# A fused sparse-attention and squared-ReLU kernel: first loads on two queues, wider mask matmuls, a re-weighted instruction planner and a last output cut by columns

## The chip, the cores and the metric

The kernel runs on one core of a Trainium2 chip. A core has a matmul engine (TensorE, "PE" in the profile, with its weight loads listed apart as "PEld"), three engines for elementwise work (VectorE "DVE", ScalarE "ACT", GpSimd "POOL") and SyncE ("SP"), which here only issues transfers. [...] semaphores order the engines against one another. The metric is device time in microseconds (us), the median of repeated executions.

## The reference

Eight batches of eight heads, 576 positions, head width 64. Half of the heads see only the last 32 positions, the other half every position with the same remainder modulo 32. The result, one row per position, goes through two matrices with s·relu(h)²+b between them.

```python
scores = scale * np.matmul(q, k.transpose(0, 1, 3, 2))
mask_local = (rel >= 0) & (rel < stride)
mask_strided = (rel >= 0) & (pos[None, :] % stride == pos[:, None] % stride)
attn = softmax(np.where(mask, scores, -1e9))     # local for heads 0-3, strided for 4-7
x = np.matmul(attn, v).transpose(0, 2, 1, 3).reshape(4608, 512)
r = np.maximum(x @ w_in, 0.0)                    # w_in 512 x 2048
out = (s * (r * r) + b) @ w_out                  # w_out 2048 x 512
```

## The kernel before

**Tiling.** Attention is done for pairs of heads: `pair_steps(b, m)`, batch `b`, pair `m` of four; pairs 0 and 1 are local, 2 and 3 strided. A pair is a list of small PE steps: transposes of q and k (L494, L502), scores (L623) with six or eight tiles, the product with v (L684), and in the early batches a transpose back (L731). Between them stand copies out of the accumulators, the exponential on ACT (L641), reciprocals and scaling (L701, L711). The first matrix product (`ff1`, L983) takes tiles of 512 tokens, nine in all, and so does the second (`ff2`, L1238, for tiles 0 and 1; `ff2_seven`, L951, for the others, which needs seven products of half matrices where eight would be usual). The last two tiles use a seven-product scheme for the first matrix as well (`ff1_seven`, L1208).

**Order of the work.** The order of instructions is made by a planner that runs when the program is built. `Plan` holds a clock and, for every piece of data, the time at which it expects it. PE steps are taken one after the other: attention steps when attention is behind its schedule (`due`, with the offset `ahead`), else `ff1` or `ff2`. Work for ACT, DVE, POOL and the transfer queues is posted and released in `flush`, in the order of the time when its data are expected plus a weight by kind (the dictionary `ORDER`; its entry `SLACK` says how far an engine's list may run ahead). What the planner expects of a transfer is an estimate: `AT` gives the landing times of the first batch, `landing` those of later ones. A wrong estimate does not make the result wrong; it puts an instruction too early into an engine's list, where it waits for its data and everything behind it waits too.

**Head of the program.** Until the first q has landed, PE runs filler matmuls (`keep_running`, L1502). SP issues the identity, two heads of the v of batch 0 in fp32 (`stage_v`, L311, into the memory that later holds `w_out_sb`) and the mask table `negs` (L315). POOL issues q, k, the other v and the weights (L345, L372, L1365, L394), converts the staged v (L404) and then goes on issuing. In batch 0 (`PE_MASK = 1`) the mask is added to the scores by PE: before each score tile, a matmul of the identity with the table writes -30000 where nothing may be seen (L620), and the score matmul accumulates on it.

**v of later batches.** `fetch_v` issues the transfers (L382, L387) and enters when the planner expects them. `rows_before` posts a copy of 32 rows within `v_loc` (L404), on ACT or DVE, whichever the planner thinks free.

**End of the program.** The last product of the last tile is P3 in `ff2_seven`. Its two token halves (t = 0 and 1) have an accumulator bank each (`Ws`); `store` scales a half into an output tile `o` on DVE (L882) and SP issues its transfer (L886).

Of the kernel before, what the change touches and what calls it, by code (L numbers as in the profile page):

```python
# [18 lines left out]
class Plan:  # L19
# [22 lines left out]
    def post(self, needs, cost, fn, keys, lat=None):  # L42
        self.pend.append((needs, cost, fn, keys, lat))

    def flush(self):
        while True:
            best = None
            for p in self.pend:
                r = self.ready_at(p[0])
                if r is None or r > self.t:  # L50
                    continue
                if p[1].keys() <= {"A", "V"} and min(
                        self.free[e] for e in p[1]) > self.t + self.SLACK:
                    continue
                k = p[3][0]
                w = r + self.LATER.get(k[0] if isinstance(k, tuple) and k[2:3] != (0,) else None, 0.0)
                if best is None or w < best[0]:
                    best = (w, r, p)
            if best is None:
                return  # L60
            _, r, p = best
            self.pend.remove(p)
            eng = min(p[1], key=lambda e: max(self.free[e], r) + p[1][e])
            end = max(self.free[eng], r, self.t - self.SLACK) + p[1][eng]
            self.free[eng] = end
            p[2](eng)
            for k in p[3]:
                if isinstance(k, Group):
                    self.banks[k.name] = end + self.LAT[eng]
                    k = ("rel", k)  # L70
                soon = isinstance(k, tuple) and k[0] == "soon"
                self.done[k] = end + (6000.0 if soon else p[4] or self.LAT[eng])
# [45 lines left out]
class Step:  # L118
    def __init__(self, fn, ns, needs=(), group=None, keys=(), posts=(), after=None):
# [3 lines left out]

ORDER = {"g": 1500.0, "S": 2500.0, "in": 2500.0, "w_mix": 0.0, "wc": 1000.0, "ev": 1000.0,
         "c21": 1500.0, "c11": 500.0, "c12": 500.0, "C22": -1500.0, "fv": 0.0, "Vb": -400.0,
         "x": -1500.0, "Ub": 1000.0, "xc": -1500.0, "fe": -400.0, "k": 1500.0, "fu": -1500.0,
         "Va": 500.0, "p": 0.0, "c22": 500.0, "Ua": 2500.0, "e": -1500.0, "q": 0.0, "r": 0.0,
         "u": 0.0, "SLACK": 600.0, "ahead": 0.05}
KINDS = ("g", "S", "in", "w_mix", "wc", "Va", "Ua", "Ub", "Vb", "C22", "xc", "q", "k", "r", "x", "e",
         "p", "u", "ev", "fv", "fu", "fe", "c11", "c22", "c21", "c12")  # L130


def varied(order, rnd):

    order = dict(order)
    for kind in rnd.sample(KINDS, rnd.choice((1, 2, 4))):
        order[kind] = rnd.choice((-1500.0, -800.0, -400.0, 0.0, 500.0, 1000.0, 1500.0, 2500.0))
    if rnd.random() < 0.2:
        order["SLACK"] = rnd.choice((400.0, 600.0, 800.0, 1000.0))
    if rnd.random() < 0.2:  # L140
        order["ahead"] = rnd.choice((0.0, 0.05, 0.1, 0.2))
    return order

# [45 lines left out]
def lay_out(ctx, tc, nc, q, k, v, moe_w_in, moe_w_out, moe_s, moe_b, out, order, q_shape, out_shape,  # L189
# [112 lines left out]
    def v_band(b, h):  # L302

        return v[b, h].rearrange("(t p) d -> p t d", p=LQ)
# [4 lines left out]
    def stage_v(heads):  # L309
        for h in heads:  # L310
            nc.sync.dma_start(out=vl_stage[LPAD:128, h], in_=v_band(0, h))  # L311

# [135 lines left out]
    PE_MASK = 1  # L448
# [25 lines left out]
    def pair_steps(b, m):  # L474
# [135 lines left out]
        def score(i, group):  # L610
# [3 lines left out]
            def f():  # L614
                if i % per_s == 0:
                    st["s", g] = bank(group)
                c = i % per_s * 2 * nq
                if b < PE_MASK:

                    nc.tensor.matmul(  # L620
                        out=st["s", g][0:nk, c:c + 2 * nq], lhsT=ident[0:nk, 0:nk],
                        rhs=neg_loc if loc else neg_str, start=True, stop=False)
                nc.tensor.matmul(  # L623
                    out=st["s", g][0:nk, c:c + 2 * nq], lhsT=(st["k"][:, i * nq:i * nq + nk] if loc else st["k"][:, i, 0:SQ]),
                    rhs=st["q"][:, i].rearrange("d e c -> d (e c)"), start=b >= PE_MASK, stop=True)

            s = Step(f, (2 if b < PE_MASK else 1) * (2 * nq / 2.4 + 8), needs=[("q", id_), ("k", id_)],
                     group=group if i % per_s == 0 else None)
            if i % per_s == n - 1:
# [28 lines left out]
            return s  # L658

        gr = None  # L660
        for i in range(nt):
            if i % per_s == 0:
                gr = group_of("s", b, m)
            steps.append(score(i, gr))

# [187 lines left out]
    def ff2_seven(T):  # L853
# [23 lines left out]

        def store(i, k, of, plus, ts=slice(0, 2)):
            def g(eng):
                o = op.tile([128, 2, 256], FP32, tag="o", name="o")  # L880
                src = gts[of, T][:, ts] if (of, T) in gts else gts[of, T, ts.start]
                nc.vector.scalar_tensor_tensor(  # L882
                    out=o[:, ts], in0=src, scalar=s_sb[:, 0:1],
                    in1=plus()[:, ts], op0=ALU.mult, op1=ALU.add)
                r0 = T * PS + 256 * i
                nc.sync.dma_start(  # L886
                    out=out[r0:r0 + 256, 256 * k:256 * k + 256].rearrange(
                        "(t p) m -> p t m", p=128)[:, ts], in_=o[:, ts])
            return g
# [50 lines left out]
        for key, group, name, fresh, lhs, rhs, needs, more, posts in seq:  # L940
            for t in range(2):
                for k in range(H):
                    halves = last and name == "W"

                    def f(k=k, t=t, group=group, name=name, fresh=fresh, lhs=lhs, rhs=rhs, key=key,
                          halves=halves):
                        if halves and fresh and k == 0:
                            gts[name, T, t] = bank(Ws[t])[:, None, 0:256]
                        elif fresh and t == k == 0:
                            gts[name, T] = bank(group).rearrange("p (t m) -> p t m", t=2)  # L950
                        nc.tensor.matmul(out=gts[name, T, t][:, 0] if halves else gts[name, T][:, t],  # L951
                                         lhsT=lhs(k, t), rhs=rhs(k),
                                         start=fresh and k == 0 and (halves or t == 0),
                                         stop=t == 1 and k == H - 1, skip_group_check=True)
                    s = Step(f, 110, needs=needs(k) + ([(x[0], T, t) if halves and x == d("C22")
                                                        else x for x in more]),
                             group=(Ws[t] if halves else group) if fresh and k == 0 and
                             (halves or t == 0) else None)
                    if k == H - 1 and key == "P3" and last:
                        s.keys = [("P3", T, t)]  # L960
                        s.posts = [([("P3", T, t)], {"V": 420.0},
                                    store(0, 1, "W", val("Ub"), slice(t, t + 1)),
                                    [Ws[t]])]
                    elif t == 1 and k == H - 1:
                        s.keys = [d(key)]
                        s.posts = posts
                    if t == 1 and k == H - 1 and key == "P3":
                        s.keys = s.keys + [("F2", T)]
# [370 lines left out]
    def fetch_v(b):  # L1339
        load_vl(b)  # L1340
        plan.done["raw", "vl", b] = landing(4600)
        for mm in range(2):
            rows_before(b, mm, ("raw", "vl", b))
        if b < LONG_V:
            early_v(b)
        else:
            load_vs(b)
            arrive(both("vs", b), landing(5000))

# [10 lines left out]
    def after_landing(i, src):  # L1360
# [9 lines left out]
    plan.free["V"] = 6500.0  # L1370
    AT = {"ql0": 5200.0, "kl0": 6900.0, "ql1": 7850.0, "kl1": 8700.0, "qs": 10200.0,
          "ks": 12100.0, "vl0": 7100.0, "vl1": 13450.0, "vs": 15000.0}
    for key, at in AT.items():
# [7 lines left out]
    nc.sync.dma_start(out=sb_row[0:1, 1:2], in_=moe_b[None, :])  # L1381
    plan.done["sb_row",] = 16000.0
    def weights_in(eng):

        nonlocal ring
        nc.gpsimd.tensor_copy(out=gate[0:8, 2:3], in_=loaded[0, "qs"][64:SQ, 0:1])
        load_w_in()
        ring = 13200.0
        for keys, cost in ([0], 2700), ([1], 2500), ([2], 2500), ([3], 2500):
# [125 lines left out]
    def due():  # L1515

        pos = f1_pos[i1] + (f2[i2 - 1].pos if i2 else 0.0) + plan.ahead
        return (pos if pos <= 1 else 1 + (pos - 1) / 2) * batch_ns

    while i2 < len(f2) or any(at_i[p] < len(att[p]) for p in range(len(att))):  # L1520
        plan.flush()
# [14 lines left out]
        if i2 < len(f2):  # L1536
            order.append(2)
        if len(order) == 2 and i1 % 4 == 0 and f1_pos[i1] > (f2[i2 - 1].pos if i2 else 0.0) + 1:
            order.reverse()
# [56 lines left out]
```

## Time and profile before

| | |
|---|---|
| median of 3 runs | 298.67 us (298.17 to 298.99) |
| the profiled execution: its own time, its span | 298.86 us, 297.1 us |
| PE busy, matmuls | 290.5 us (98%), 2802 |
| DVE, ACT, POOL busy | 235.3, 194.3, 93.7 us |
| PE clock granted | 0.999 of full |
| transferred | 38.19 MB, mean 129 GB/s |

The span goes from the first to the last instruction; 1.8 us of the execution's time lie outside it. PE is shown as busy nearly always, but its busy time is modelled and overlapping, so idle PE time is better read from the starts of consecutive matmuls: a 128x256 matmul in a dense stretch starts 109 ns after the one before, a 128x512 one 216 ns. "issue" in the chain of waits is time in which the engine waits for nothing that the profile shows.

### The profile page before, as it was taken

To read this page: it belongs to the slowest core of one execution; us is meant where nothing else is said; L and a number is where in the kernel's file an instruction comes from. 1 tells how busy PE (TensorE), PEld (TensorE's weight loads), DVE (VectorE), ACT (ScalarE), POOL (GpSimd) and SP (SyncE) were. 2 spreads that over 40 slices of the span, in tenths; PEclk is the share of its full clock that TensorE was granted. 3 is DMA by queue.
4 is the path that set the end of the run, shared out by engine and by line. 5 is a ranking of instruction groups with operands and counts; after the bars stand their busy time and mean duration, and the time that the engine had idled before them with its cause. 6 is when DMAs were issued, how large, how long until landed. Compare 5 with 4: busy or idle time off the path is not lost.

```text
span 297.1 us, 7092 instructions
## 1 busy us (share of the span) xinstructions
PE 290.5 (98%) x2802; PEld 220.0 (74%) x2802; DVE 235.3 (79%) x501; ACT 194.3 (65%) x336; POOL 93.7 (32%) x140
## 2 busy tenths in 40 slices
PE   8999999999999999999999999999999999999995
PEld 3775656666556568889767776768888989999984
DVE  5857888798966988787877896759898588888963
ACT  3577957898838798647774878469877545675400
POOL 8873624601980296009710394100000000000000
PEclk9999999999999999999999999999999999999999
DMA  8999999997999499989999999999230300110214
GB/s 136 189 206 203 218 180 184 223 171 119 109 195 149 67 132 138 170 173 122 148 136 144 182 170 105 143 140 207 44 97 0 108 29 9 71 38 3 95 48 142
DMA packets 106152, 38.19 MB, mean 129 GB/s; under 512 B 85414, under 2 KB 103974, under 8 KB 106118
## 3 DMA queue, kind: packets, MB, share of 16 engines
q0 software_dynamic: 60848, 18.23, 62.7%
q1 hardware_dynamic: 45270, 19.51, 36.0%
q8 instruction: 22, 0.36, 0.5%
q14 instruction: 12, 0.10, 0.1%
HBM read 36.99 MB, written 10.62 MB: 160 GB/s over the span
## 4 chain that ended last, share of the span: by engine, by line
PE 88%; DMA 6%; ACT 2%; DVE 2%; POOL 1%; issue 1%; ACTq 0%
PE ps_f L983 28%; PE ps_f L951 22%; PE ps_f L1238 8%; DMA v_loc<-in_v_dram 6%; PE ps_s L623 5%; PE ps_f L1208 3%; PE ps_a L684 3%; PE ps_s L1502 2%; PE ps_a L1208 2%; PE ps_s L951 2%; PE ps_t L1208 2%; PE ps_s L1208 2%; PE ps_t L951 1%; PE ps_s L1238 1%; PE ps_t L684 1%; PE ps_t L502 1%
## 5 line engine op out<-in xcount | busy, mean ns | idle before, releaser
L983 PE MATMUL ps_f<-xT,w_in_sb 128*128 128x512 f16 (+4 forms) x568 | 115.5, 331 | 0.3 <-ACT u L1009 0.3
L1009 ACT ACTIVATE u<-ps_f 128x512 f16<-128x512 f32 x104 | 61.0, 594 | 32.5 <-PE ps_f L983 31.8
L983 PEld LDWEIGHTS <-w_in_sb 128*128 128x128 f16 x576 | 57.4, 114 | 23.2 <-issue 0.5
L951 PEld LDWEIGHTS <-gT 128*128 128x128 f16 x608 | 58.4, 98 | 9.2
L951 PE MATMUL ps_f<-w_out_sb,gT 128*128 128x256 f16 x376 | 55.6, 273 | 0.0
L1017 ACT ACTIVATE gT<-u 128x1024 f16<-128x1024 f16 x29 | 30.7, 1057 | 0.8
L1238 PE MATMUL ps_f<-w_out_sb,gT 128*128 128x512 f16 x112 | 30.4, 379 | 0.0
L951 PE MATMUL ps_f<-w_mix,gT 128*128 128x256 f16 x176 | 25.1, 273 | 0.0
L641 ACT ACTIVATE p_str<-ps_s 72x432 f16<-72x432 f32 (+1 forms) x46 | 20.7, 482 | 6.4 <-PE ps_s L623 5.8
L711 DVE TENSOR_TENSOR x_nat<-ps_a,rec 96x384 f16<-96x384 f32 (+2 forms) x46 | 24.1, 523 | 0.6
L641 ACT ACTIVATE p_loc<-ps_s 128x384 f16<-128x384 f32 x46 | 21.4, 494 | 4.8 <-PE ps_s L623 4.3
L1019 DVE TENSOR_TENSOR gT<-u 128x1024 f16<-128x1024 f16 x27 | 18.5, 686 | 5.9 <-ACT u L1009 5.4
L819 DVE TENSOR_TENSOR gT<-gT 128x1024 f16<-128x1024 f16 x34 | 22.4, 678 | 0.6 <-ACT gT L1017 0.4
L382 POOL DMA_DIRECT2D v_loc<-in_v_dram x24 | 17.7, 757 | 8.6 <-DMA w_out_sb<-in_moe_w_out_dram 5.7
L951 PEld LDWEIGHTS <-S 128*128 128x128 f16 x176 | 17.1, 98 | 2.9
L1238 PEld LDWEIGHTS <-gT 128*128 128x128 f16 x128 | 11.4, 98 | 7.8
L387 POOL DMA_DIRECT2D v_str<-in_v_dram x16 | 13.0, 816 | 12.3 <-PE ps_f L983 3.6
L684 PEld LDWEIGHTS <-p_str 72*128 72x128 f16 x256 | 12.8, 98 | 5.1 <-ACT p_str L641 0.4
L1323 POOL COPY gate<-kT 1x1 f16<-1x1 f16 x6 | 1.5, 256 | 45.0 <-DMA kT<-ks 45.0
L951 PE MATMUL ps_f<-w_mix,S 128*128 128x256 f16 x112 | 15.5, 273 | 0.0
L701 DVE RECIPROCAL rec<-ps_a 96x6 f32<-96x6 f32 (+2 forms) x47 | 8.6, 182 | 8.6 <-PE ps_a L684 8.4
L1149 ACT ACTIVATE gT<-u 128x1024 f16<-128x1024 f16 x12 | 12.7, 1058 | 1.7 <-DVE u L1128 1.4
(237 smaller groups left out, 529.7 us busy)
## 6 DMA issues: line engine op xcount, KB each, us to landing
out_dram<-o SPq DMA_DIRECT2D x34, 256.0 KB, 2.9
w_in_sb<-in_moe_w_in_dram POOLq DMA_DIRECT2D x4, 512.0 KB, 9.7
w_out_sb<-in_moe_w_out_dram POOLq DMA_DIRECT2D x4, 512.0 KB, 9.9
qs<-in_q_dram POOLq DMA_DIRECT2D x6, 288.0 KB, 8.4
ks<-in_k_dram POOLq DMA_DIRECT2D x6, 288.0 KB, 9.7
v_loc<-in_v_dram POOLq DMA_DIRECT2D x24, 72.0 KB, 9.6
ql<-in_q_dram POOLq DMA_DIRECT2D x4, 288.0 KB, 9.0
kl<-in_k_dram POOLq DMA_DIRECT2D x16, 72.0 KB, 3.6
```

What stands on the lines that cost most here:

```text
L382: nc.gpsimd.dma_start(out=vl[LPAD:128, h, :, 0:D], in_=v_band(b, h))
L641: nc.scalar.activation(out=st["pw", g][0:nk, 0:2 * n * nq], in_=st["s", g][0:nk, 0:2 * n * nq], func=AF.Exp, scale=scale)
L684: nc.tensor.matmul(out=st["pa", g][:, n % 6, :], lhsT=st["pw", gp_][0:nk, i * nq:i * nq + WIDE], rhs=vt[0:nk, 2 * mm + e, j, :])
L711: nc.vector.tensor_tensor(out=x_at(0, cnt), in0=st["pa", g][0:nq, 0:cnt, 0:D], in1=st["rec", g][0:nq, 0:cnt].to_broadcast([nq, cnt, D]), o ...
L819: {"V": nc.vector, "P": nc.gpsimd}[eng].tensor_tensor(out=at(out), in0=at(x), in1=at(y), op=op)
L951: nc.tensor.matmul(out=gts[name, T, t][:, 0] if halves else gts[name, T][:, t], lhsT=lhs(k, t), rhs=rhs(k), start=fresh and k == 0 and (ha ...
L983: nc.tensor.matmul(out=gts["h", T, ft][:, lo:hi], lhsT=w_in_sb[ft // 4][:, ct].rearrange("p (x l) -> p l x", l=4)[:, ft % 4], rhs=xT[ct][: ...
L1009: nc.scalar.activation(out=u, in_=gts["h", T, ft], func=AF.Relu)
L1017: nc.scalar.activation(out=g, in_=u, func=AF.Square)
L1019: nc.vector.tensor_tensor(out=g, in0=u, in1=u, op=ALU.mult)
L1208: nc.tensor.matmul(out=st[bk][:, 256 * t:256 * t + 256], lhsT=lhs(t, c), rhs=rhs(c), start=fresh and t == c == 0, stop=t == c == 1, skip_g ...
L1238: nc.tensor.matmul(out=gts[id_], lhsT=gts[T][:, ft, ts * 128:(ts + 1) * 128], rhs=w_out_sb[:, ft, cols], start=(ft == 0), stop=(ft == NFT ...
```

## The change

1. `stage_v`: head 0 of the staged v is issued from ACT's queue, head 1 stays on SP and so follows the identity directly; the mask table follows it.
2. Mask matmuls of batch 0: a new step `forbid` writes the mask of a whole accumulator bank at once (two local tiles, three strided ones), and stands ahead of the first score of that bank. It needs the table, neither q nor k. There are 12 of them where there were 28.
3. `fetch_v`: for the last batch alone the planner expects v 5 us later than before.
4. The last P3: the second token half is computed and stored in two halves of 128 columns, one after the other in the same bank. The pieces of an output tile share one `o`.
5. The planner: nearly all weights in `ORDER` differ, `SLACK` is 400 instead of 600, single items of batch 0 have weights of their own (`late`), `ahead` has an offset for each of six stretches of the work, `lead` (how far the first product may run ahead of the second) is 1.1 instead of 1, and `AT` holds earlier landing times.

```diff
-            nc.sync.dma_start(out=vl_stage[LPAD:128, h], in_=v_band(0, h))
+            queue = nc.sync if h else nc.scalar
+            queue.dma_start(out=vl_stage[LPAD:128, h], in_=v_band(0, h))
...
-                if b < PE_MASK:
-
-                    nc.tensor.matmul(
-                        out=st["s", g][0:nk, c:c + 2 * nq], lhsT=ident[0:nk, 0:nk],
-                        rhs=neg_loc if loc else neg_str, start=True, stop=False)
...
+        def forbid(i, group):
+
+            n = min(per_s, nt - i)
+
+            def f():
+                st["s", i // per_s] = bank(group)
+                nc.tensor.matmul(
+                    out=bank(group)[0:nk, 0:2 * n * nq], lhsT=ident[0:nk, 0:nk],
+                    rhs=(neg_loc if loc else neg_str)[:, None, :].to_broadcast([nk, n, 2 * nq]),
+                    start=True, stop=False, skip_group_check=True)
+            return Step(f, 2 * n * nq / 2.4 + 3, needs=[("negs",)], group=group)
...
-        def store(i, k, of, plus, ts=slice(0, 2)):
+        def store(i, k, of, plus, ts=slice(0, 2), ms=slice(0, 256)):
             def g(eng):
-                o = op.tile([128, 2, 256], FP32, tag="o", name="o")
+                if (of, T) in gts or (i, k, "o") not in gts:
+                    gts[i, k, "o"] = op.tile([128, 2, 256], FP32, tag="o", name="o")
+                o = gts[i, k, "o"]
...
+            ends = [(t, k, slice(0, 256)) for t in range(2) for k in range(H)]
+            if last and key == "P3":
+                ends = ends[0:H] + [(1, k, slice(128 * c, 128 * c + 128)) for c in range(2)
+                                    for k in range(H)]
...
-                    s = Step(f, 110, ...
+                    s = Step(f, 110 if ms.stop - ms.start == 256 else 57, ...
...
-        plan.done["raw", "vl", b] = landing(4600)
+        late = 5000.0 if b == B - 1 else 0.0
+        plan.done["raw", "vl", b] = landing(4600) + late
...
-            arrive(both("vs", b), landing(5000))
+            arrive(both("vs", b), landing(5000) + late)
...
-    AT = {"ql0": 5200.0, "kl0": 6900.0, "ql1": 7850.0, "kl1": 8700.0, "qs": 10200.0,
-          "ks": 12100.0, "vl0": 7100.0, "vl1": 13450.0, "vs": 15000.0}
+    AT = {"ql0": 5000.0, "kl0": 6300.0, "ql1": 7200.0, "kl1": 8000.0, "qs": 9700.0,
+          "ks": 11700.0, "vl0": 7100.0, "vl1": 13000.0, "vs": 14500.0}
...
         pos = f1_pos[i1] + (f2[i2 - 1].pos if i2 else 0.0) + plan.ahead
+        pos += order_.get(f"ahead{int(pos / 3)}", 0.0)
```

## The prediction

> **What bounds the kernel now.** First the busy table of the page, then the starts of consecutive matmuls, then the chain of waits where those starts show a gap, and last the two ends.
>
> ```profile
> PE 290.5 (98%) x2802; PEld 220.0 (74%) x2802; DVE 235.3 (79%) x501; ACT 194.3 (65%) x336; POOL 93.7 (32%) x140
> ```
>
> PE sets the time. From about 20.4 us to its last matmul, which starts at 293.30, its spacing is the streaming time (109 ns for 256 columns, 216 for 512) but for a few gaps: 0.15 us at 174.95, 0.51 at 196.03, 0.58 at 199.92, 0.40 at 239.20. So the change can gain in three places only: before 20 us, in these 1.6 us of gaps, and after the last matmul. The chain of waits tells what made the two large gaps:
>
> ```profile
> 178.55 16.76 DMA v_loc<-in_v_dram
> 195.31 0.02 issue
> ...
> 195.39 0.12 ACT v_loc L404
> 195.51 0.51 issue
> 196.02 0.59 ACT u L1009
> ...
> 199.12 1.06 ACT gT L1017
> 200.18 0.39 ACT p_loc L641
> ```
>
> The v of batch 7 lands at 195.31, and the copy of its rows stands in ACT's list before that. ACT's own timeline has it:
>
> ```profile
> 195.39 0.73 ACT L404 COPY v_loc<-v_loc 32x640 f16<-32x640 f16 x1 [2.47 <-DMA v_loc<-in_v_dram]
> ```
>
> ACT idles 2.47 us; the `u` behind it frees late the bank that PE needs (first gap), and the backlog delays an exponential (second). The product that needs this v runs only at 202.36.
>
> At the head, in a table by stretch, the fillers (L1502) and the transfers matter:
>
> ```profile
> 1.50:2.50 1.00, 1.00 (x4) 0.41 (x3) 0.83 (x5) 0.81 (x1) 1.00 (x2) 1.00 0.28 65
> 3.00:4.00 1.00, 1.00 (x3) 0.30 (x2) 0.86 (x3) 0.00 (x0) 1.00 (x3) 1.00 1.11 149
> 6.00:8.00 2.00, 2.00 (x26) 1.28 (x25) 0.34 (x1) 1.27 (x2) 2.00 (x4) 1.00 1.25 193
> ```
>
> The last two numbers are the busy share of the DMA engines and GB/s: they are mostly idle until 2.5 us and full from then on. PE's useful streaming from 5.33 to 20 us is only 9.2 us; 2.8 are fillers and 3.1 gaps. DVE is the chain from 7.66 to 14.8 us, with 0.83 us idle in it:
>
> ```profile
> 1.14 1.00 SPq L311 DMA_DIRECT2D w_out_sb<-in_v_dram  x2
> 2.18 0.52 SPq L315 DMA_DIRECT2D w_mix<-negs  x1
> 7.66 0.76 DVE L404 COPY kT_loc<-ps_a 128x576 f16<-128x576 f16 x1 [1.74 <-PE ps_a L494]
> 8.39 1.81 POOL L404 CAST v_loc<-w_out_sb 128x384 f16<-128x384 f32 x3
> 14.77 2.27 POOL L404 COPY v_str<-vs 72x512 f16<-72x512 f16 x4 [0.59 <-DMA vs<-in_v_dram]
> ```
>
> At the tail, one scaling follows the last matmul, and its transfer issues at 294.13:
>
> ```profile
> 292.54 1.04 PE L951 MATMUL ps_f<-w_out_sb,S 128*128 128x256 f16 x8
> 293.61 0.48 DVE L882 SCALAR_TENSOR_TENSOR o<-ps_f,sb_all,Ub 128x256 f32<-128x256 f32 x1 [0.39 <-PE ps_f L951]
> ```
>
> [...] The trace agrees (109 and 216 ns; 56 for 128 columns): fewer, wider matmuls of the same columns save some 3 ns each. [...]
>
> **The change part by part.** The sums are made against the profiled execution (298.86, span 297.1); the median is 0.19 lower.
>
> *v of the last batch late.* The planner's list moves the row copies of batch 7 later, by 5 us of its clock. ACT's 2.47 us wait and both gaps go: 0.51 + 0.58 = -1.09 us. What is late next: the second half of v (transfer landed 201.94) is used at 207.95, so it is not. The copy itself (0.73 us) must end before 202.36; with a start near 197 to 200 it does.
>
> *First loads.* Before, SP issues at 0.74 (identity), 1.14 and 1.64 (v), 2.18 (mask). After, head 0 goes to ACT, which is free from 0.68 until its table load at 1.69 (1.28 us, first used at 6.06, so a delay of about 0.45 us, the first v issue's duration, is hidden). Head 1 starts at 1.14, the mask at 1.64: each about 0.5 us earlier, in DMA time that was idle (share 0.28). From 2.5 us the engines are full, so all that follows lands about 0.5 us earlier: k of the first heads, 6.70, at about 6.2, and strided v, 14.62, at about 14.1. `AT` moves by 0.2 to 0.7 us, so PE's order can use it. DVE's chain then starts 0.5 us earlier, and so do POOL's casts of strided v, behind which the last products of batch 0 stand (16.80). POOL's issues themselves (to 8.45) and its first cast (to 10.20) do not move: that bounds the gain for pair 0, whose v product runs at 10.15. I take -0.54; ends 0 and -1.2 (the fillers and DVE's idle time a better order could use as well).
>
> *Wide masks.* Before: 12 x 83 ns + 16 x 65 ns = 2.04 us on PE. After: 6 x 163 (384 columns, as L983 has them) + 4 x 182 + 2 x 122 (432 and 288 columns[...]) = 1.95. -0.09 us. The first mask of pair 0 can replace fillers (0.16); those of later pairs stood before their copies' end already (at 11.26 and 13.72). I take -0.08 in all; ends 0 and -0.3. No instruction waits behind a mask for longer: the table is issued by 1.64 and first needed after 7 us.
>
> *Halved last output.* In the old plan the second half's eight matmuls start at 292.54 (call it S), the last at S+0.76, DVE starts 0.31 later and ends at S+1.55. New: 16 matmuls of 128 columns at 56 ns, one bank. A scaling of 128 columns: 512 takes 0.75, 256 takes 0.48, so 0.345 us by extrapolation. By the planner's own rule a result counts as ready 200 ns after its last matmul, so about four of the second quarter's eight matmuls (57 ns each) are written ahead of the first quarter's scaling, and four behind it. If the bank orders them, DVE starts after the fourth (S + 11 x 0.056 + 0.26 = S+0.88), ends at S+1.22; PE resumes at about S+1.29, its last matmul starts at S+1.46, the last scaling starts at S+1.72 and ends at S+2.07: +0.52. The last transfer is half as large (its data take 0.37 us before), which gives back about 0.10. Sum +0.42. If nothing orders them: S + 0.84 + 0.26 + 0.345 = S+1.45, -0.10, and with the transfer -0.2. I take +0.42, as no part of a bank is read during its filling anywhere else here. SP's issues, 0.45 us each, lie apart by more than that.
>
> *The planner.* Weights, `SLACK`, `lead` and `ahead` move most instructions, but PE's total of useful columns stays. Where PE is dense it can gain only the gaps at 174.95 and 239.20 (0.55 us), and can lose by new ones: bounds -0.55 and about +2.5. I take 0: the same planner left no gap above 0.15 us between 23 and 174 us before, two behind an fp32 matmul at 49 us apart.
>
> Sum: -1.09 - 0.54 - 0.08 + 0.42 = -1.29; 298.86 - 1.29 = 297.57, and for the median 298.67 - 1.29 = 297.4.
>
> **The rivals.**
> *A, forecast:* 297.4 (0.42), own range 296.9 to 297.9.
> *B, the last bank isn't ordered,* or the planner puts the first scaling behind all matmuls: 297.4 - 0.6 = 296.8 (0.18). For it: the program's regions are disjoint. [...]
> *C, the head's gain is hidden:* POOL's chain of issues, cast (10.20) and weights (10.38 on) sets batch 0, and earlier loads wait. Then 297.4 + 0.54 = 297.9 to 298.0 (0.22), about no change. For it: the cast at 8.39 follows POOL's issues with no wait for a transfer. Against: DVE's idle 1.74 us before 7.66 waits for k.
> *D, slower:* the pace offset. Over positions 6 to 9 of 18 `ahead` falls from +0.05 to -0.15; a position is about 270/18 = 15 us, so attention may slip 3 us. Batch 7's q and k are fetched from 169.08 on, once batch 5 is far enough; its transposed k lands at 196.60 and is used at 198.61: 2.0 us of cover. A slip L beyond that stops PE for L - 2.0. It decides at L = 2.0 + 1.3 + 0.9 = 4.2 us; at L = 5 the time is 297.4 + 3.0 = 300.4. For it: DMA share 1.65 from 180 to 200 us, so nothing catches up. Against: over positions 9 to 12, where the fetch lies, the offset is +0.05 as before, and the planner lays the scores by the fetch. 0.18, taken at 300.
> That the late v does nothing (another copy or relu waits in the same place) is in C and D.
>
> **How the numbers follow.** 0.3% is 0.90 us, about what a measurement can tell: faster is below 297.77, slower above 299.57. A gives 0.36 faster, 0.06 same; B 0.18 faster; C 0.07 faster, 0.14 same, 0.01 slower; D 0.03 same, 0.15 slower. Together 0.61, 0.23, 0.16. The range 296.0 to 299.5: below lie B with the head's -1.2, above most of D.
>
> **What would show it.** ACT's copy of v_loc without a wait, and no gap from 195 to 201. SP's second issue a v, k's landing near 6.2, the first kT copy near 7.1. The last four matmuls after a pause of about 0.65 us, DVE's first quarter scaling ahead of them. Dense PE from about 19.9. Wrong would be a gap over 1 us between 25 and 290, or no shift of strided v's cast.

## The result

| | before | after |
|---|---|---|
| median | 298.42 us (297.88 to 298.99, 6 runs) | 301.53 us (300.05 to 303.30, 6 runs) |
| profiled execution: time, span | 298.86, 297.1 us | 302.25, 300.5 us |
| first q landed | 4.89 us | 7.14 us |
| last matmul starts | 293.30 us | 296.00 us |
| last scaling ends | 294.10 us | 296.60 us |

The kernel is slower: ratio 1.0106, interval 1.0067 to 1.0145, where 297.4 us was forecast. The medians here and below are of the executions within 1.5% of the fastest of the same kernel; that leaves out two of six in e13 and one each in e4, e12 and e14. The busy table hardly moves; PE has 8 matmuls fewer and is busy for a smaller share:

```profile
PE 289.8 (96%) x2794; PEld 219.0 (73%) x2794; DVE 240.8 (80%) x505; ACT 190.5 (63%) x329; POOL 91.2 (30%) x139
```

To see where the time went I count, at equal amounts of PE work done (fillers left out), how much later the kernel after stands than the kernel before. It is +1.36 us at 25 us, +1.42 from 52 to 175, +1.26 behind 175 (the small gap there is gone), +0.16 at 203, +1.03 behind 204, +0.64 behind 240 (that gap is gone too), and +2.70 at the last matmul. So there are two losses, at the head and at the tail, and a gain at 195 to 201 of which most is lost again at 203.

**Head.** The same three stretches of the kernel after. The last two numbers are again the busy share of the DMA engines and GB/s:

```profile
1.50:2.50 1.00, 1.00 (x4) 0.41 (x3) 0.84 (x5) 0.81 (x1) 1.00 (x2) 1.00 0.71 162
3.00:4.00 1.00, 1.00 (x3) 0.30 (x2) 0.86 (x3) 0.00 (x0) 1.00 (x3) 1.00 1.02 140
6.00:8.00 2.00, 0.82 (x16) 0.62 (x16) 0.00 (x0) 0.33 (x1) 0.64 (x2) 1.00 1.25 192
```

The idle DMA time ahead of 2.5 us is used now (0.71 where 0.28 was), as forecast. But between 6 and 8 us PE does 16 matmuls where it did 26 and DVE nothing at all. The timelines of the engines give the reason (start, duration, instruction, idle time before it and what ended that):

```profile
0.74 0.39 ACTq L340 DMA_DIRECT2D w_out_sb<-in_v_dram  x1
...
1.14 0.45 SPq L340 DMA_DIRECT2D w_out_sb<-in_v_dram  x1
1.64 0.50 SPq L344 DMA_DIRECT2D w_mix<-negs  x1
...
7.18 0.45 PE L523 MATMUL ps_t<-ident,ql 96*64 96x96 f16 x12 [2.00 <-DMA ql<-in_q_dram]
...
7.71 0.90 POOL L1412 DMA_DIRECT2D v_loc<-in_v_dram  x1 [1.36 <-DMA ql<-in_q_dram]
9.77 1.76 POOL L433 CAST v_loc<-w_out_sb 128x384 f16<-128x384 f32 x3
...
15.33 2.37 POOL L433 COPY v_str<-vs 72x512 f16<-72x512 f16 x4 [0.59 <-DMA vs<-in_v_dram]
```

PE and POOL both wait for the first q. Before, POOL issued the same transfer without a wait:

```profile
6.33 0.95 POOL L1365 DMA_DIRECT2D v_loc<-in_v_dram  x1
```

On POOL the wait of 1.36 us stands ahead of this issue, and what follows is late by about as much: the cast starts at 9.77 (8.39 before), the first weights land at 18.33 (17.10). The trace also tells why this issue waits for q. POOL's first eight transfers mark their landing in eight semaphores in turn, numbers 99 to 106; the load of v_loc is the ninth and takes the one of the first q, 99, again. POOL's wait for 99 ends at 7.16, q landed at 7.14. The same wait stands in the kernel before, where it was over at 4.91.

**Middle.** In ACT's timeline of the kernel after the row copy of v no longer waits:

```profile
198.90 0.73 ACT L433 COPY v_loc<-v_loc 32x640 f16<-32x640 f16 x1
```

Both gaps are gone. In the chain of waits of the same kernel a new one stands a little later, before the strided scores:

```profile
185.27 12.01 DMA v_str<-in_v_dram
...
197.35 6.94 DMA kT<-ks
204.29 0.04 issue
204.33 0.57 PE ps_s L647 x6
```

SP issues the transposing transfer of k at 197.35; it lands 6.9 us later, and PE stands still for 0.84 us.

**Tail.** First PE's timeline, then DVE's:

```profile
293.10 0.83 PE L997 MATMUL ps_f<-w_out_sb,S 128*128 128x128 f16 x12
295.83 0.38 PE L997 MATMUL ps_f<-w_out_sb,S 128*128 128x128 f16 x4 [1.89 <-DVE o L923]
```

```profile
294.38 0.75 DVE L923 SCALAR_TENSOR_TENSOR o<-ps_f,sb_all,Ua 128x512 f32<-128x512 f32 x1 [2.94 <-DMA out_dram<-o]
295.05 0.47 DVE L923 SCALAR_TENSOR_TENSOR o<-ps_a,sb_all,Ub 128x256 f32<-128x256 f32 x1
295.44 0.34 DVE L923 SCALAR_TENSOR_TENSOR o<-ps_f,sb_all,Ub 128x128 f32<-128x128 f32 x1
296.25 0.35 DVE L923 SCALAR_TENSOR_TENSOR o<-ps_f,sb_all,Ub 128x128 f32<-128x128 f32 x1 [0.48 <-PE ps_f L997]
```

The last four matmuls come after a pause, and DVE's first quarter stands ahead of them: the bank is ordered, as forecast. But from the twelfth matmul's start to the next there are 2.11 us instead of about 0.65, because DVE is late. The scaling of the product before it waited 2.94 us until an earlier output had left its tile `o`, of which there are three. Before, this scaling waited for PE alone:

```profile
291.87 0.75 DVE L882 SCALAR_TENSOR_TENSOR o<-ps_f,sb_all,Ua 128x512 f32<-128x512 f32 x1 [1.00 <-PE ps_f L951]
```

Why did that output take so long? The view of the DMA queues, before from 288 to 292 us and after from 290 to 294, cuts the stretch into 40 slices of 0.1 us. Before:

```profile
GB/s 0 0 0 0 0 164 0 0 0 0 0 0 0 0 0 0 0 0 0 0 0 0 0 133 338 328 338 164 164 328 348 348 134 0 0 0 0 10 256 369
q8 instruction: 1, 0.02, 1.9%
```

After:

```profile
GB/s 0 0 0 0 0 0 0 0 0 215 512 317 267 92 266 317 348 246 41 0 0 0 0 0 0 0 0 10 10 10 10 10 10 20 21 20 113 348 348 358
q8 instruction: 1, 0.02, 2.7%
```

Before, a single packet stands at 288.55, alone; the outputs follow from 290.3 on. It is 16 KB of instructions, on a queue of its own (`q8`). After, it starts at 291.00, in the first slices of the outputs, and takes 1.75 us (1.23 before). Behind the outputs nothing else starts for 0.8 us (the bytes of a packet are counted where it starts), and then there is a trickle of 10 GB/s for another 0.9. The single packets of the trace show what the trickle is: it starts at 292.73, just where the fetch ends (291.00 + 1.75), and consists of packets of 1 KB one after the other, eight of them, then one of 4 bytes, then more. The landings show the delay too: each output's is marked in sixteen steps. For the output that was issued at 290.06, fifteen steps came 1.55 to 1.73 us after the issue and the last one at 3.87, which is 293.93, 0.49 us behind the start of the first 4-byte packet; for the same output before, all sixteen came by 1.74. For the next output, issued at 290.50, fifteen came by 1.77 and the last at 3.75. DVE's waits for the two end at 293.95 and 294.28, each within 0.03 us of the last step. (The records don't name the DMA engine of a packet, so what kept the last steps back until the fetch had ended is not shown; the times are. In e1, e2, e3, e7 and e13, too, a slow packet of 1 KB starts within 0.02 us of the fetch's end.)

### The profile page after: what moved, and what is told of

Its sections match the earlier page's. It is cut to its first block, busy times and chain, and to the rows that moved or that the text cites. A ratio compares the mean times of both kernels' runs of the same rounds, so it can differ in the third digit from the quotient of the medians.

```text
span 300.5 us, 7083 instructions
## 1 busy us (share of the span) xinstructions
PE 289.8 (96%) x2794; PEld 219.0 (73%) x2794; DVE 240.8 (80%) x505; ACT 190.5 (63%) x329; POOL 91.2 (30%) x139
## 4 chain that ended last, share of the span: by engine, by line
PE 79%; DMA 13%; DVE 3%; issue 1%; POOL 1%; ACT 0%; SPq 0%; DVEq 0%; POOLq 0%
PE ps_f L1029 27%; PE ps_f L997 19%; PE ps_f L1284 8%; DMA v_str<-in_v_dram 4%; PE ps_s L647 4%; DMA ks<-in_k_dram 3%; PE ps_f L1254 3%; PE ps_a L723 2%; DMA kT<-ks 2%; DMA out_dram<-o 2%; DMA ql<-in_q_dram 2%; PE ps_t L1254 2%; PE ps_a L1254 2%; PE ps_s L997 2%; PE ps_s L1254 2%
## 5 line engine op out<-in xcount | busy, mean ns | idle before, releaser
L997 PE MATMUL ps_f<-w_out_sb,gT 128*128 128x256 f16 x376 | 57.1, 273 | 0.0
L1065 DVE TENSOR_TENSOR gT<-u 128x1024 f16<-128x1024 f16 x31 | 21.2, 684 | 7.3 <-ACT u L1055 6.9
L1063 ACT ACTIVATE gT<-u 128x1024 f16<-128x1024 f16 x25 | 26.4, 1058 | 0.7
L750 DVE TENSOR_TENSOR x_nat<-ps_a,rec 72x384 f16<-72x384 f32 (+2 forms) x47 | 24.7, 525 | 0.7
L740 DVE RECIPROCAL rec<-ps_a 72x6 f32<-72x6 f32 (+2 forms) x47 | 8.6, 183 | 8.3 <-PE ps_a L723 8.1
L858 DVE TENSOR_TENSOR S<-gT 128x1024 f16<-128x1024 f16 x18 | 11.8, 681 | 0.0
```

Source lines behind the costliest of these rows:

```text
L750: nc.vector.tensor_tensor(out=x_at(0, cnt), in0=st["pa", g][0:nq, 0:cnt, 0:D], in1=st["rec", g][0:nq, 0:cnt].to_broadcast([nq, cnt, D]), o ...
L858: {"V": nc.vector, "P": nc.gpsimd}[eng].tensor_tensor(out=at(out), in0=at(x), in1=at(y), op=op)
L997: nc.tensor.matmul(out=dst[:, ms], lhsT=lhs(k, t), rhs=rhs(k)[:, ms], start=fresh and k == 0 and (halves or t == 0), stop=t == 1 and k == ...
L1063: nc.scalar.activation(out=g, in_=u, func=AF.Square)
L1065: nc.vector.tensor_tensor(out=g, in0=u, in1=u, op=ALU.mult)
```

## The experiments

Theories: (1) v on ACT's queue delays the first q, and that is the +1.3 of the head; (2) the tail's loss is the halved last output, by its bank or by its shared tile; later, when that did not hold, (3) it is the instruction fetch among the outputs, which the mask matmuls moved there.

| kernel | median, us | ratio to before, interval | first q lands | matmuls behind the last fetch | DVE's longest wait for an output at the end |
|---|---|---|---|---|---|
| before, measured along with each | 298.4 to 298.7 | | 4.89 | 44 | none |
| after | 301.53 | 1.0067 to 1.0145 | 7.14 | 35 | 2.94 |
| after, v on SP (e1) | 299.95 | 1.0037 to 1.0067 | 5.40 | 27 | 2.99 |
| after, old tail (e2) | 300.38 | 1.0032 to 1.0074 | 6.31 | 19 | 2.65 |
| after, v on SP, old tail (e3) | 299.13 | 1.0010 to 1.0055 | 5.35 | 26 | 2.63 |
| before, v on ACT (e4) | 299.31 | 0.9995 to 1.0037 | 6.01 | 44 | none |
| before, new tail (e5) | 299.02 | 0.9999 to 1.0036 | 5.17 | 49 | none |
| before, halves in own tiles (e6) | 300.41 | 1.0042 to 1.0084 | 5.22 | 48 | 1.59 |
| e3 with four tiles (e7) | 297.64 | 0.9965 to 0.9994 | 5.79 | 22 | 0.59 |
| e3 with 27 more fillers (e8) | 297.65 | 0.9943 to 0.9981 | 4.75 | 53 | none |
| before, late v (e9) | 299.63 | 1.0015 to 1.0047 | 5.48 | 43 | none |
| e8 with four tiles (e12) | 297.77 | 0.9946 to 0.9986 | 4.92 | 54 | none |
| before, wide masks (e13) | 302.48 | 1.0095 to 1.0196 | 5.58 | 27 | 2.26 |
| before, v on ACT later (e14) | 299.27 | 0.9998 to 1.0049 | 6.32 | 45 | none |
| after, more fillers (e15) | 299.53 | 0.9992 to 1.0038 | 5.95 | 63 | none |
| e15, v on SP (e16) | 298.14 | 0.9968 to 1.0024 | 5.39 | 62 | none |

The last three columns are from the one profiled execution of each.

**1. After with v on SP (e1).**

```diff
-            queue = nc.sync if h else nc.scalar
-            queue.dma_start(out=vl_stage[LPAD:128, h], in_=v_band(0, h))
+            nc.sync.dma_start(out=vl_stage[LPAD:128, h], in_=v_band(0, h))
```

> The changed kernel with both staged heads of v on SP's queue as before; all else, the planner's order too, as changed. Theory 1 (the head was lost because the transfers of the two hardware queues now run ahead of the first q): the first q lands near 4.9 us, PE's first transposes start near 5.3 instead of 7.18, and the time falls by about 1.3 us, to 300.2. Rival (the head was lost by the planner's new order and its earlier landing times): the first q still lands near 7 or batch 0 is still late by 1.3 us, and the time stays near 301.5.

The first q lands at 5.40, and the list stands within 0.1 us of before at the head. 299.95: 1.6 us of the 3.1 come from ACT's queue. The tail's wait stays, 2.99 us. (The interval of the kernel after is 1.2 us to either side, so such a difference of medians is rough.)

**2. After with the old last output (e2), and 3. with both undone (e3).**

```diff
-                if (of, T) in gts or (i, k, "o") not in gts:
-                    gts[i, k, "o"] = op.tile([128, 2, 256], FP32, tag="o", name="o")
-                o = gts[i, k, "o"]
+                o = op.tile([128, 2, 256], FP32, tag="o", name="o")
...
-            if last and key == "P3":
-                ends = ends[0:H] + [(1, k, slice(128 * c, 128 * c + 128)) for c in range(2)
-                                    for k in range(H)]
...
-                                    {"V": 480.0 if ms.stop - ms.start == 256 else 280.0},
+                                    {"V": 420.0},
```

> The changed kernel with the last output as before: no column halves, an output tile per piece. Theory 1 (the tail was lost by the ordered bank and the shared output tile): the gap of 2.1 us before the last four matmuls goes, and with it 2.1 us of PE plus 0.4 of DVE and about 0.9 of the last transfers: 301.5 - 2.8 = 298.7, at least below 299.5. Rival (a slow transfer of that one execution made the tail, not its code): the time stays within 0.6 us of the changed kernel's.

> Both undone; what is left of the change is wide masks, the late v and the planner's new order. If the two losses add: 301.5 - 1.3 - 2.8 = 297.4, faster than before by 1.0 us. If the planner's new order loses time of its own: above 298.4.

e2 gains 1.2 us of the 2.8 that were expected. Theory 2 fell here. In e3 neither the halves nor the shared tile are left, the last matmul starts 1.81 us earlier than before, and the kernel is still slower than before: DVE waits 2.63 us for an output that took 3.88 us to land, where the same output took 1.74 before.

**4. Before with v on ACT (e4).**

```diff
-            nc.sync.dma_start(out=vl_stage[LPAD:128, h], in_=v_band(0, h))
+            queue = nc.sync if h else nc.scalar
+            queue.dma_start(out=vl_stage[LPAD:128, h], in_=v_band(0, h))
```

> The kernel before with the first staged head of v on ACT's queue and nothing else. Theory 1: the first q lands near 7.1 us and the time rises by 1.0 to 1.5 us, to about 299.7. Rival: the queue alone does nothing: the first q lands within 0.4 us of 4.9 and the time is 298.1 to 298.8.

The first q lands 1.12 us later, the list is 0.67 us late at the head and 0.76 at the end; the median is 0.9 above before, with an interval that just reaches no change. The DMA queues from 0 to 4 us, before and e4 (packets, MB, share; `q0` is POOL's queue, which brings q; `q1` is SP's, `q10` ACT's):

```profile
q0 software_dynamic: 160, 0.12, 24.8%
q1 hardware_dynamic: 810, 0.20, 23.0%
```

```profile
q1 hardware_dynamic: 747, 0.19, 22.7%
q0 software_dynamic: 59, 0.05, 18.1%
q10 hardware_dynamic: 592, 0.15, 16.3%
```

By 4 us the identity, v and the mask have moved 1,339 packets instead of 810, and POOL's queue 59 instead of 160. Over all profiled executions: with v on SP alone, POOL's queue has moved 92 to 175 packets by then and the first q lands at 4.75 to 5.79 (eleven of them); with v on ACT, 59 to 86 packets, and 5.95 to 7.14 (five). The groups do not overlap; within the second, the count does not order the landings (86 packets in the latest and in the earliest). POOL's load of v_loc follows: it is issued at 6.29 to 6.38 in the eleven, and in the five at 6.52 to 7.71, each time 0.57 us after the first q landed.

**5. Before with the new last output (e5), and 6. with halves in tiles of their own (e6).** e5 adds to the kernel before the parts removed in e2; e6 the same without the shared tile.

> The kernel before with the whole new last output (column halves in one bank, pieces sharing an output tile) and nothing else. Theory 1 (ordered bank and shared tile): DVE's first quarter stands before the last four matmuls, which wait for it; the shared tile makes the scaling of the product before wait for two transfers instead of one. Last DVE scaling 1.0 to 1.9 us later, one more transfer issue at the end: 298.4 + 1.8 = 300.2 (299.4 to 300.8). Rival (the tail loses only where a slow transfer happens to stand, as in the changed kernel's execution): 298.2 to 299.0.

> The kernel before with the column halves in one bank, but an output tile for every piece. Theory 1a (the ordered bank alone): a gap of about 0.6 us before the last four matmuls, last scaling 0.5 us later, one more transfer: 298.9 to 299.3. Theory 1b (the bank is nothing, the shared tile is all): no gap, 298.2 to 298.6.

PE and DVE of e5 at the end:

```profile
293.93 0.38 PE L958 MATMUL ps_f<-w_out_sb,S 128*128 128x128 f16 x4 [0.44 <-DVE o L884]
```

```profile
294.36 0.35 DVE L884 SCALAR_TENSOR_TENSOR o<-ps_f,sb_all,Ub 128x128 f32<-128x128 f32 x1 [0.48 <-PE ps_f L958]
```

The bank costs what was forecast: the last scaling ends 2.05 us after the second half's first matmul at 292.66 (2.07 forecast), 0.6 us later than before, and no output is waited for. The 300.2 us that were expected of the bank and the shared tile did not come: 299.02. In e6, at 300.41 where 298.9 to 299.3 was expected, the last quarter takes a fourth tile and has to wait for the first one's transfer. So the shared tile helps:

```profile
295.49 0.35 DVE L882 SCALAR_TENSOR_TENSOR o<-ps_f,sb_all,Ub 128x128 f32<-128x128 f32 x1 [1.59 <-DMA out_dram<-o]
```

**7. A fourth output tile (e7), 8. more filler instructions (e8), 12. both (e12),** each on e3.

```diff
-    op = ctx.enter_context(tc.tile_pool(name="op", bufs=3))
+    op = ctx.enter_context(tc.tile_pool(name="op", bufs=4))
```

```diff
+        pieces = [1] * n if plan.t < 4900.0 else [n]
...
-            nc.tensor.matmul(
-                out=out, lhsT=ones16, rhs=ones16[:, None, :].to_broadcast([128, n, 128]),
-                start=True, stop=True)
+            for p in pieces:
+                nc.tensor.matmul(
+                    out=out[:, 0:128 * p], lhsT=ones16, rhs=ones16[:, None, :].to_broadcast([128, p, 128]),
+                    start=True, stop=True)
```

> The changed kernel with v on SP and the old last output, and four output tiles instead of three. Theory 2 (with masks, late v and new order PE ends 1.8 us early, but the last scalings wait for an earlier output's transfer to free its tile, here 2.6 us): that wait goes, the last scaling follows the last matmul as before, and the time is 298.4 - 1.7 = 296.7 to 297.2. Rival (the last transfers themselves are slow, a fourth tile only moves the wait into them): 298.0 to 299.1, as without it.

> The changed kernel with v on SP and the old last output; the filler matmuls of the first 4.9 us are cut into pieces of 128 columns, the same columns in all. That adds 54 instructions to PE's list at a place where PE only waits. Theory 3 (the slow transfer is an instruction fetch of 16 KB for PE that the 32 missing mask instructions moved from before the last outputs into them): the fetch stands about 2.9 us earlier against PE's end, the first of the last outputs lands 1.8 us after its issue instead of 3.9, the wait of 2.6 us goes: 296.7 to 297.3. Rival (the order or the transfers make it, not the fetch): the wait stays, 298.3 to 299.3.

> The kernel after with both heads of v on SP, the old last output, finer fillers (54 more instructions on TensorE, which bring the last instruction fetch ahead of the outputs) and a fourth output tile. Theory: both remedies act on the same wait for output transfers, so together they give what each gives, 297.3 to 297.7. Rival (each leaves part of the wait): below 297.2.

Either remedy takes 1.5 us off e3, and both are faster than before, though some 0.4 us above the ranges that were expected. The fourth tile shortens the wait, though the fetch is still at 290.73 among the outputs:

```profile
292.98 0.48 DVE L920 SCALAR_TENSOR_TENSOR o<-ps_a,sb_all,Ub 128x256 f32<-128x256 f32 x1 [0.59 <-DMA out_dram<-o]
```

The 54 instructions (27 matmuls, each with its weight load) in the first 5 us, a time in which PE waits anyway, move the fetch to 286.42, ahead of the outputs, and nothing waits. Together they give no more than one of them (297.77): both act on one wait. The best kernel is e7 or e8, 0.2 to 0.4% below before.

**9. Before with the late v alone (e9).** The two lines of the diff in `fetch_v`, nothing else.

> The kernel before with the last batch's v planned 5 us later, nothing else. The list of instructions on TensorE keeps its length, so all that lies at the end should stay. Theory of the prediction (ACT's 2.47 us wait makes both gaps at 196.03 and 199.92): ACT's row copy of v without a wait, no gap from 195 to 201, time 298.4 - 1.1 = 297.3. Rival (another late item stands in the same place, or the gain is given back by the slot of the instruction fetch among the last outputs, which now meets outputs that are 1.1 us earlier): gaps gone in the trace, but DVE's last scalings wait for an output transfer, time 298.0 to 298.6.

Both gaps are gone, but at the end the list is 1.69 us late. The rival's "another late item" is right; which one, neither text named. The chain of waits:

```profile
191.74 10.79 DMA qT<-qs
202.53 0.02 issue
202.55 0.67 ACT qD_str L404
...
203.93 0.50 ACT p_loc L641
204.43 0.04 issue
204.47 0.35 PE ps_s L623 x3
```

The transposed strided q, issued at 191.74, lands at 202.5. ACT's copy of it, not v's, now stands ahead of the exponentials, and PE loses 1.23, 0.20 and 0.25 us from 203 to 206.5. Another 0.93 goes at 231.43, where DVE's list has another order than before. So v was only the first of several transfers that are due between 195 and 205 us.

**13. Before with wide masks alone (e13).** The two parts of the diff with `forbid`, and the time at which the planner expects the table.

> The kernel before with one mask matmul per accumulator bank, nothing else: 16 matmuls and 16 weight loads fewer. Theory of the instruction fetch: the 16 KB transfer on an extra queue, at 288.55 before, comes some 32 to 34 instructions of work later, at about 290 to 291, among the transfers of the last outputs; one of these takes over 3 us where it took 1.8, a scaling of the last outputs waits for it, time 299.0 to 299.6. Rival (the masks are worth what the sum says, and the fetch is harmless): no wait of DVE on an output transfer, time 298.35 +- 0.3.

302.48, some 3 us more than theory 3 asked for. The fetch starts at 292.95, with 27 matmuls to go instead of 44. DVE's timeline, and the slices of 0.1 us from 292 to 296 us:

```profile
295.64 0.75 DVE L892 SCALAR_TENSOR_TENSOR o<-ps_f,sb_all,Ua 128x512 f32<-128x512 f32 x1 [2.26 <-DMA out_dram<-o]
```

```profile
GB/s 0 0 0 0 0 0 0 0 82 492 328 297 174 133 328 317 317 144 10 0 0 0 0 10 10 10 10 10 10 20 21 20 143 348 358 328 348 358 338 318
```

It is the picture of the kernel after: burst, nothing, trickle, and again the trickle's first packet starts at 294.35, where the fetch ends (292.95 + 1.41). The rest of this kernel's loss is the planner's: 0.9 us ahead of 83.57 (ACT's `gT` now stands behind an exponential that it preceded before), 0.9 ahead of 233.31, at the place of e9's last loss, and 1.9 at 195.16, where v's copy waits for its transfer on ACT for longer than before. ACT's timeline:

```profile
195.92 0.73 ACT L404 COPY v_loc<-v_loc 32x640 f16<-32x640 f16 x1 [3.87 <-DMA v_loc<-in_v_dram]
```

**14. Before with v on ACT, later (e14).** The edit of e4, and ahead of it on ACT a copy of one element, in front of which the table load stands (and, earlier than before, the `memset` of the tile that it reads).

> The kernel before with head 0 of the staged v on ACT's queue, but behind ACT's table load and a copy of one element, so that it is issued at about 3.1 us; no instruction is added to TensorE, and none leaves it. Theory of the early bytes (what delays the first q is that v and the mask table lie ahead of it by 2 us): the first q lands at or before 4.9, PE's first transpose of it at 5.3, time 298.4 +- 0.4, the cast of the staged v at 8.4. Rival (a third queue that is active at the same time is what delays it, whenever it is issued): the first q lands at 6 us or later, and the time is 299.0 to 299.6.

The first q lands at 6.32. But the case it was made for did not come about: the trace has ACT's queue issue v at 1.04, while the table load (0.73 to 2.01) still ran and ahead of the copy (2.03), behind which it stands in the program. So v was issued only 0.3 us later than in e4. (The other work did keep to the program's order in the kernel before: all 335 instructions of ACT without its table load, 501 of DVE and 140 of POOL start in it.) Whether a v on a second queue that comes behind q would leave q alone was not tried.

**15. After with more fillers (e15), and 16. with v on SP too (e16).** The edit of e8 on the kernel after and on e1.

> The kernel after with its first fillers cut into 128-column pieces (54 more instructions on TensorE), nothing else: v on ACT's queue and the halved last output stay. Theory of the instruction fetch: the fetch of 291.0 comes ahead of the last outputs, the pause before the last four matmuls falls from 2.11 to the 0.5 to 0.65 us that the ordered bank costs, and the time from 301.5 to about 299.9; the first q stays at 6 us or later. Rival (the pause is made by the halved output and its shared tile): the pause stays above 1.5 us, time 301 to 302.

> The same with both heads of v on SP, the halved last output kept. Theory: first q at 5 us, no wait of the last outputs; against the same kernel with the old last output (297.65) it pays the ordered bank alone, +0.4 to +0.6: 298.1. Rival (without the fetch the halved output is worth its smaller last transfer): 297.3 to 297.6.

This settles the tail in the kernel after itself. PE's timeline of e15:

```profile
292.51 0.83 PE L997 MATMUL ps_f<-w_out_sb,S 128*128 128x128 f16 x12
293.78 0.38 PE L997 MATMUL ps_f<-w_out_sb,S 128*128 128x128 f16 x4 [0.44 <-DVE o L923]
```

The fetch is at 287.38 now. The pause falls from 2.11 to 0.66 us from start to start, no output is waited for, and the last output lands 1.57 us after its issue instead of 2.22. These are 2.1 us together; the median falls by 2.0. e16, at 298.14, is before within its interval.

In this way the medians take the kernel after apart, each step known to about 1 us and without the parts being quite independent: 301.53; without the fetch among the outputs 299.53; without ACT's queue as well 298.14; with the old last output as well 297.65 (e8), which leaves -0.8 for the wide masks, the late v and the new plan.

## Why the prediction was wrong

Two steps failed. The first loads, taken at -0.54 us, cost 1.36 in the profiled execution. And the wide masks, taken to have no effect beyond their own time, moved an instruction fetch into the last outputs, which cost about 2.0 (after against e15). A third term, the next late transfer behind v, was taken at nothing and was 0.87 in the profiled execution.

**First loads: wrong in sign.** The step said that v and the mask would fill idle DMA time and that "all that follows lands about 0.5 us earlier", -0.54. They did fill it, yet the first q landed 2.25 us later, and the head lost 1.36 us in the trace and 0.9 to 1.6 in the medians (e4 against before, e3 against e2, e16 against e15, e1 against after). The step assumed one line of transfers in which q stands behind v. They run side by side: before, SP's queue started 810 packets from 1.72 to 4.00 us, and POOL's 160 from 2.85 on. On SP alone the two heads of v and the mask are one queue, with ACT they are two, and q's is a third; by 4 us POOL's queue has then moved 59 to 86 packets. Whether the second queue is the cause, or merely that v and the mask come half a microsecond earlier, no run shows, since e14 did not separate the two. In either case the time saved on issue was not all that the edit changed. The rival C (no gain at the head) was nearer, and it too expected no loss. And the bound "POOL's issues do not move" was false: the ninth waits for the landing of the first q, whose semaphore it takes again, and that wait was in the program before as well. (The head's three shares of PE time, 9.2, 2.8 and 3.1 us, add up to 15.1 in a stretch of 14.7; nothing in the sum rests on them.)

**Wide masks: their own time right, their side effect missed.** They take 1.99 us of PE instead of the forecast 1.95: 187 and 126 ns for 432 and 288 columns, for which the forecast had estimates (182 and 122) that lie on the line through the measured 109 ns for 256 columns and 216 for 512. What the step did not see is that 16 matmuls fewer, and as many weight loads, move the last instruction fetch against the end of PE's list. The traces have 22 fetches of 16 KB in each kernel, the last four on average 123 to 131 matmuls apart (some records are missing), and the last one when 2,757 to 2,767 matmuls have started, in all sixteen kernels. So in these kernels the length of the list says where it falls: before, 44 of 2,802 matmuls are left behind it, after, 35 of 2,794. Where at most 35 matmuls were left behind it, DVE waited 2.3 to 3.0 us for an output with three tiles; with 43 or more it did not wait, but for e6, which needs a fourth tile. In the kernel after, the fetch among the outputs cost about 2.0 us (e15), in the sum 0: the prediction's "No instruction waits behind a mask for longer" looked at the masks' own place alone.

**Halved last output: the bank right, the sum in part by luck.** +0.6 in e5, 0.5 between e16 and e8, for a forecast of +0.42; the pause was 0.66 us for a forecast 0.65. That the bank orders the halves was an assumption of the forecast; the traces show it read and written in turn: in the kernel after DVE's first quarter ends at 295.78 and PE goes on at 295.83, in e5 at 293.88 and 293.93. But in e5 the smaller last transfer gives back more than the 0.10 that was taken: it lands 1.66 us after its issue instead of 2.04. And a cost that no one had named takes about as much: from the last landing to the end of the span it is 1.35 to 1.36 us in the six kernels with the halved output and 0.92 to 0.93 in the ten others. At the end SP goes through the landing semaphores one after the other, 0.06 us each. The last output's is the last of them before; with one transfer more the last output takes a semaphore that is second in this order, and seven more checks stand behind its landing. The step also left out how long a transfer holds its tile: "SP's issues lie apart" looked at issues alone. In the kernel after they did not even lie apart: the last scaling ends at 296.60, and its transfer is issued at 296.90, behind the issue at 296.42.

**v of the last batch late: right in what goes, wrong in what is late next.** The gaps went, -1.10 us as summed. The step looked for the next late item in v alone. It was the transposed k: 0.84 us came back at 203 in the profile of after. The prediction's rival D had named that place and its 2.0 us of cover, but tied it to the pace offset. Alone on the kernel before the edit loses (e9). In the plan of after it holds: e1, e2, e3, e7, e8, e12 and e16 show no gap from 176 to 285 us, e15 one of 0.4. And which transfer is last differs between executions of one list. e6 and e14, whose lists are that of before up to the end or throughout, stood at 196 and 200 as before did; e5, also that list, stood at 203.0 and 204.8 (1.15 us in all), and e4 at 205 (0.5 us). So the -1.09 was the size of two gaps that three of these five executions have.

**Planner: 0 in the sum, and about that in the middle.** The gaps at 174.95 and 239.20 went, -0.15 and -0.40, and no other over 0.2 us came between 52 and 203.

The sum of the trace: +1.36 head, +0.06 to 52 us, -0.15, -1.10, +0.87, -0.40, and +2.06 at the tail makes +2.70 at the last matmul. The smaller last scaling gives back 0.19, the late issue costs 0.27, the last transfer lands 0.18 later behind its issue, and SP's checks cost 0.44: +3.40, the difference of the spans. Of the four terms of the forecast, three came near their size (-1.09, -0.08, +0.42; the masks' own time fell by 0.05, and the +0.42 was a sum of wrong parts) and one had the wrong sign; the 0.87 at 203 and the some 2 us of the fetch were in none.

## What to carry to other kernels

Here a gap that waited for a transfer was worth its length only where the next transfers in the same stretch were early enough: of 1.09 us, 0.84 came back at 203. Look at all that are due within a few microseconds of it, and at how they share the DMA engines, before the whole gap is put into a sum. The second queue for early loads was no free gain: with it the first q landed at 5.95 to 7.14 us instead of 4.75 to 5.79. Count the packets that the first needed tensor has got by the time it is wanted. And an edit that took 16 matmuls off PE left 27 behind the last instruction fetch instead of 44 (e13): count from the last fetch to the end of the list, and see which transfer it meets and how many buffers stand ready while that transfer is under way.

## What was not expected of the hardware

A fetch of 16 KB of instructions is one packet, and the last one of each kernel took 0.93 to 1.75 us, while the data of a 128 KB output take 0.4, an estimate from the 340 GB/s of the slices above. When it met the outputs, one of them took 3.5 to 3.9 us to land instead of at most 1.8, with fifteen of its sixteen landing steps in time (in the kernel after, by 1.73 us). The packets behind the fetch were slow too: in the kernel after, 0.08 to 0.14 us for the first six, 0.04 to 0.05 for most others. A change of 16 matmuls in the first 18 us of a kernel cost about 2 us in its last 10 (after against e15). And one output transfer more put 0.43 us of checks behind the last landing.
